# Two weight chunks of a fused attention and MoE kernel converted at earlier places of the first stage

## The chip, the cores and the metric

The kernel runs on one core of one Trainium2 chip. The metric is the device time of one execution in microseconds (us), lower is better. Before the change it is 903.88 us, the median of three runs (903.26 to 904.88).

## The reference

For each of 4 batch entries ("inputs" below) and 8 heads, random-feature attention over 576 positions; then two feed-forward layers, each of them two matrix products with a gate between:

```python
# per head: q, k, v are 576 x 64, omega is 128 x 64
def phi(x):
    h = x @ omega.T - (x * x).sum(-1, keepdims=True) / 2
    return np.exp(h - h.max(-1, keepdims=True)) / np.sqrt(128)
q_p, k_p = phi(q * 64**-.25), phi(k * 64**-.25)
attn = (q_p @ (k_p.T @ v)) / (q_p @ k_p.sum(0) + 1e-6)
x = attn, heads side by side             # 2304 x 512
h = x @ moe_w_in                         # 512 x 2048
x = (h * np.clip(h + 3, 0, 6) / 6) @ moe_w_out
h = x @ moe2_w_in
out = (h / (1 + np.exp(-1.702 * h))) @ moe2_w_out
```

All tensors are float32, and the weights of the two layers arrive in a raw form that the kernel converts on the chip: each chunk goes through a short chain of bit operations and arithmetic, and is then split into a high and a low part, so that one product becomes three matmuls.

## The kernel before

**Stages.** Attention makes x, one input after another; each input has 512 main positions and 64 leftover ones, its 8 heads are held in 4 pairs. The first feed-forward layer is walked in units of (input, chunk), with 16 chunks of 128 hidden columns: `emit_h` multiplies x by the chunk of w_in (line 513, 12 matmuls: 4 blocks of x, one for each pair of heads, by 3), gates the result and splits it, and `emit_o` multiplies it by the chunk of w_out two units later (line 555). The attention of the next input is issued in small steps between the units. The second layer runs last (lines 856 to 1008).

**The steps of one input's attention** (`att_steps`). For head h: PJ(h) projects keys and queries on the features (line 289) and calls `features`, which takes the negated maximum on VectorE (line 295, two per head) and the exponentials on ScalarE (line 297, eight per head); QT(h) transposes the query features, with a copy by VectorE for the first input (line 372); KV(h) sums keys by values and copies the sum by ScalarE (line 363); NU(h) makes the numerator (line 386), and `norm` divides on VectorE (lines 413 to 421); XT(i) transposes a finished pair into one block of x (line 433), split by ScalarE and VectorE (lines 279, 280). For the first input there are 41 steps. The order is PJ(h), NU(h-2), QT(h-1), KV(h-1), and XT(i) after each second head. The loads of a later pair are issued with KV of the odd heads.

**Converting a chunk.** `load_w` loads the raw words of a chunk, two transfers of 512 KB, into one of two buffers `wraw`. `convert_1` does two ScalarE passes (lines 213 and 215), three VectorE passes (lines 217, 221, 225) and one GpSimd multiplication (line 228). `convert_2` adds two halves on VectorE (line 236), copies each to its high part on ScalarE (line 239) and subtracts for the low part on VectorE (line 240); what does not stay resident is stored (line 242). `convert_next(stage, upto, act, dve)` does all conversions up to number `upto` that are not done yet, and then `prefetch_w` issues the raw loads of the two chunks after the last one begun. The buffers `wtop`, `wmag` and `wpow` are single in the first layer, `w` is double.

**What sets the order.** The kernel is written with a planner that gives each instruction to its engine's queue ahead of time, by the order of the program text, by data and buffers, and by its own estimate of durations; at run time each engine takes its queue in that order. An instruction can be planned ahead of earlier text when its inputs are there. `behind(ins)` (line 115) adds one rule: what is issued in its block, and stands on the same engine as `ins`, comes after `ins` in that engine's queue. All loads and stores of this stage are in the one queue of SP, in order.

**Around the change** (lines 743 to 750), while the first input's 41 steps are issued: after the first step at which the third pair of heads (0, 2) has been asked for, that is after KV(1), the raw words of chunks 0 and 1 are asked for, behind that pair's v on SP. Ahead of step 29, KV(5), chunk 0 is converted, with its first ScalarE pass behind the last exponential of the fifth head, its second behind that of the sixth, and its VectorE passes behind the maximum of the fifth head. Chunk 1 is converted after `emit_h(0, 0)`, behind the eighth head's exponentials, chunk 2 after `emit_h(0, 1)`, and so on, `min(c + 2, NC)` chunks after unit c of the first input. From step 29 on the attention of this input takes its PSUM banks from the four of `acc`, and the four of `psp` are left to `emit_h`.

Of the kernel before, what the change touches and what calls it, by code (L numbers as in the profile page):

```python
# [22 lines left out]
def performer_moe_kernel(  # L23
# [26 lines left out]
    NC, _, DM = w1_out.shape  # L50
# [3 lines left out]
    LAG = 2  # L54
    TAIL = 12
    WARM = 8
    FIRST = 4
    ASIDE = 2
    PAIRED = 2
    HELD = 8  # L60
# [54 lines left out]
    def behind(*ins):  # L115
        stack = ExitStack()
        for i in ins:
            if i is not None:
                stack.enter_context(tc.issue_after(i.ins))
        return stack  # L120
# [4 lines left out]
    qkv = {}  # L125
# [74 lines left out]
    def convert_1(l, c, act=None, dve=None):  # L200
        t = wraw.pop((l, c)).rearrange("p (w s) -> p w s", s=4)
        n = 2 * DM
        top = t[:, 1:n + 1, 0]
        mid = t.rearrange("p w s -> p (w s)").bitcast(U32).rearrange("p (w s) -> p w s", s=2)[:, 0:n, 1]
        a = wp.tile([P, n], BF16, tag=f"wtop{l and c % 2}", bufs=1, name="wtop")
        m = wp.tile([P, n], BF16, tag="wmag", bufs=1, name="wmag")
        q = wp.tile([P, n], BF16, tag="wpow", bufs=1, name="wpow")
        w = wp.tile([P, n], F32, tag="w", bufs=2, name="w")

        ab, mb, qb = a.bitcast(I32), m.bitcast(I32), q.bitcast(I32)  # L210
        act = act if isinstance(act, tuple) else (act, act)
        with behind(act[0]):
            nc.scalar.activation(out=a, in_=top.bitcast(BF16), func=AF.Copy, scale=2.0 ** -112)  # L213
        with behind(act[1]):
            nc.scalar.activation(out=w, in_=mid, func=AF.Copy, scale=2.0 ** -36)
        with behind(dve):
            nc.vector.tensor_scalar(
                out=mb, in0=ab, scalar1=3, scalar2=0x7FF87FF8,
                op0=ALU.logical_shift_left, op1=ALU.bitwise_and,
            )  # L220
            nc.vector.scalar_tensor_tensor(  # L221
                out=ab, in0=ab, scalar=-0x7FFF8000, in1=mb,
                op0=ALU.bitwise_and, op1=ALU.bitwise_or,
            )
            nc.vector.tensor_scalar(  # L225
                out=qb, in0=ab, scalar1=-0x7F0080, scalar2=None, op0=ALU.bitwise_and
            )
        nc.gpsimd.tensor_tensor(out=w, in0=w, in1=q, op=ALU.mult)  # L228
        half[l, c] = a, w

    def convert_2(l, c, dve=None):
        a, w = half.pop((l, c))
        for j, kind in enumerate("io"):
            wj = w[:, j * DM:(j + 1) * DM]
            with behind(dve if l == 1 else None):
                nc.vector.tensor_tensor(out=wj, in0=wj, in1=a[:, j * DM:(j + 1) * DM], op=ALU.add)  # L236
            if l == 0:
                s = ws[l, kind, c] = ws_tile(kind, c)
                nc.scalar.copy(s[:, 0], wj)  # L239
                nc.vector.tensor_tensor(out=s[:, 1], in0=wj, in1=s[:, 0].bitcast(F32), op=ALU.subtract)  # L240
                if (l, kind, c) in ws_dram:
                    nc.sync.dma_start(out=ws_dram[l, kind, c], in_=s.bitcast(F32))
        if l == 1:
            whole[c] = w.rearrange("p (k o s) -> p k o s", k=2, o=2)
# [451 lines left out]
    n_load = [0]  # L696
    n_conv = [0, 0]

    def convert_next(stage, upto, act=None, dve=None):

        while n_conv[stage - 1] < min(upto, len(conv)):
            if stage == 1:
                prefetch_w()
                convert_1(*conv[n_conv[0]], act, dve)
            else:
                convert_next(1, n_conv[1] + 1, act, dve)
                convert_2(*conv[n_conv[1]], dve)
            n_conv[stage - 1] += 1
        prefetch_w()

    def prefetch_w():
        while n_load[0] < min(len(conv), n_conv[0] + 2):
            load_w(*conv[n_load[0]])
            n_load[0] += 1
# [25 lines left out]
    att = Att(0, xblk[0], xl)  # L740
    steps = att_steps(att)
    for i, st in enumerate(steps):
        if i == len(steps) - TAIL:
            banks[0] = "acc"
            (a0, d0), (a1, _) = att.feat[FIRST], att.feat[FIRST + 1]
            convert_next(2, 1, (a0, a1), d0)
        st()
        if n_load[0] == 0 and (0, 2) in qkv:
            with behind(last_load[0]):
                prefetch_w()  # L750
    banks[0] = "ps"
# [55 lines left out]
    for u in range(len(units) + LAG):  # L807
        while fetches and fetches[0][0] <= u + AHEAD:
            fetch_w(0, *fetches.pop(0)[1:])
        if u < len(units):  # L810
# [21 lines left out]
            if (n, c) == (B - 1, PREP):  # L832
                assert n_late[0] == len(late)
                prep, _ = x_ops(0, wp, "w")
# [410 lines left out]
```

## Time and profile before

| | us |
|---|---|
| device time, median of three runs | 903.88 |
| device time of the profiled execution | 906.58 |
| its span, first to last instruction | 904.8 |
| TensorE busy (share of the span) | 886.0 (98%) |
| VectorE busy | 554.3 (61%) |
| ScalarE busy | 478.0 (53%) |
| GpSimd busy | 322.6 (36%) |

In the rows PE is TensorE's matmuls, PEld its weight loads, DVE VectorE, ACT ScalarE, POOL GpSimd, SP the queue that issues the loads and stores. L213 is line 213 of the kernel before. A bracket behind a row of the timeline is the idle time of that engine just before the row, and what ended it. An engine that was idle cost nothing unless TensorE, which is busy 98% of the span, had to wait for it.

### The profile page before, as it was taken

The numbers are of one execution on the slowest core, as the hardware profiler recorded it, in microseconds if no ns is written. First come the engines' busy times: TensorE is split into PE (matmuls) and PEld (weight loads), VectorE is DVE, ScalarE is ACT, GpSimd is POOL, SyncE is SP. The second block draws the span as 40 slices with busy tenths as digits, with TensorE's granted clock in tenths as the row PEclk, the third lists the DMA queues.
The fourth block names the chain that finished last, engine by engine and source line by source line (L and its number), as shares of the span: only waits on it lengthen the run. The fifth ranks groups of instructions, "written<-read, shape, count | busy, mean of one in ns | idle before, by whom it ended". The sixth has DMA issues, their size and how long they took to land.

```text
span 904.8 us, 16525 instructions
## 1 busy us (share of the span) xinstructions
PE 886.0 (98%) x6344; PEld 757.1 (84%) x6344; DVE 554.3 (61%) x952; ACT 478.0 (53%) x973; POOL 322.6 (36%) x257
## 2 busy tenths in 40 slices
PE   8899999999999999999999999999999999999998
PEld 6667777788788778878888888878999888899998
DVE  5887688473754736475573343666887343368785
ACT  5887677376664666656553343444545232245452
POOL 0122222044636565475673121877000243440000
PEclk9999999999999999999999999999999999999999
DMA  6677669698888987778857325999889644565562
GB/s 209 226 248 270 234 239 316 245 329 282 286 275 288 342 304 290 233 276 288 314 204 256 128 98 206 349 400 356 277 288 354 233 170 162 180 174 153 158 204 82
DMA packets 74416, 224.57 MB, mean 248 GB/s; under 512 B 7521, under 2 KB 13793, under 8 KB 74337
## 3 DMA queue, kind: packets, MB, share of 16 engines
q1 hardware_dynamic: 73872, 223.12, 71.1%
q8 instruction: 50, 0.82, 0.4%
q10 hardware_dynamic: 464, 0.39, 0.2%
q14 instruction: 30, 0.24, 0.1%
HBM read 160.57 MB, written 62.91 MB: 247 GB/s over the span
## 4 chain that ended last, share of the span: by engine, by line
PE 82%; DVE 8%; ACT 6%; issue 1%; POOL 1%; DMA 1%; DVEq 0%; SPq 0%; ACTq 0%; POOLq 0%
PE o L1008 19%; PE o L555 18%; PE ps L513 18%; PE h L856 16%; PE hl L873 3%; PE ps L289 2%; ACT e L297 2%; DVE w L236 2%; PE ps L386 1%; PE ps L347 1%; ACT wtop L213 1%; DVE mx L295 1%; DVE wtop L221 1%; PE ps L369 1%; DVE gs L530 1%
## 5 line engine op out<-in xcount | busy, mean ns | idle before, releaser
L513 PE MATMUL ps<-x,wss 128*128 128x512 f32 x768 | 195.5, 399 | 2.5 <-ACT el L297 1.1
L1008 PE MATMUL o<-wss,gs 128*128 128x256 f32 x1512 | 173.9, 277 | 0.2 <-DVE gs L977 0.2
L1008 PEld LDWEIGHTS o<-wss,gs 128*128 128x128 f32 x1512 | 173.4, 188 | 0.9 <-DVE gs L977 0.6
L513 PEld LDWEIGHTS ps<-x,wss 128*128 128x128 f32 x768 | 140.9, 189 | 35.0 <-ACT wss L239 3.1
L856 PE MATMUL h<-xo,wss 128*128 128x512 f32 x672 | 158.5, 391 | 0.9 <-DVE t L889 0.9
L856 PEld LDWEIGHTS h<-xo,wss 128*128 128x128 f32 x672 | 123.9, 188 | 27.5 <-DVE t L889 1.8
L228 POOL TENSOR_TENSOR w<-w,wpow 128x1024 f32<-128x1024 f32 x32 | 69.2, 2162 | 204.6 <-DVE wpow L225 166.7
L525 DVE SCALAR_TENSOR_TENSOR ga<-ga,ps 128x512 f32<-128x512 f32 x80 | 50.1, 632 | 121.1 <-ACT ga L524 121.1
L899 POOL TENSOR_TENSOR g<-g,c 128x512 f32<-128x512 f32 x48 | 64.7, 1349 | 164.0 <-ACT g L898 163.8
L976 ACT CAST gs<-g 128x512 fp32r<-128x512 f32 x112 | 69.6, 622 | 80.3 <-PE o L1008 49.3
L555 PE MATMUL o<-gs,wsh 128*128 128x512 f32 (+1 forms) x480 | 110.4, 374 | 1.2 <-ACT gs L529 1.0
L555 PE MATMUL o<-gs,wss 128*128 128x512 f32 (+1 forms) x480 | 109.5, 374 | 0.2 <-ACT gs L529 0.2
L253 POOL TENSOR_TENSOR wsn<-w,wsn 128x512 fp32r<-128x512 f32 x64 | 86.6, 1367 | 63.5 <-ACT wsn L252 63.5
L977 DVE TENSOR_TENSOR gs<-g,gs 128x512 fp32r<-128x512 f32 x112 | 79.9, 716 | 33.6 <-ACT gs L976 32.3
L524 ACT ACTIVATE ga<-ps,three 128x512 f32<-128x512 f32 x80 | 51.4, 650 | 86.5 <-PE ps L513 86.0
L555 PEld LDWEIGHTS o<-gs,wsh 128*128 128x128 f32 x480 | 82.2, 188 | 17.6 <-ACT gs L529 1.4
L555 PEld LDWEIGHTS o<-gs,wss 128*128 128x128 f32 x480 | 82.4, 188 | 15.8 <-ACT gs L529 0.4
L297 ACT ACTIVATE e<-ps,mx 128x128 f32<-128x128 f32 x220 | 61.1, 396 | 23.5 <-DVE mx L295 23.3
L530 DVE TENSOR_TENSOR gs<-ga,gs 128x512 fp32r<-128x512 f32 x80 | 62.5, 791 | 16.5 <-ACT gs L529 14.7
L898 ACT ACTIVATE g<-c 128x512 f32<-128x512 f32 x48 | 30.3, 632 | 60.2 <-DVE c L889 60.2
L529 ACT CAST gs<-ga 128x512 fp32r<-128x512 f32 x80 | 46.0, 580 | 27.8 <-DVE ga L525 27.4
L252 ACT CAST wsn<-w 128x512 fp32r<-128x512 f32 x64 | 38.3, 620 | 39.5 <-DVE w L236 13.2
(132 smaller groups left out, 1102.7 us busy)
## 6 DMA issues: line engine op xcount, KB each, us to landing
wss<-left SPq DMA_DIRECT2D x56, 512.0 KB, 3.9
wss<-ws0i SPq DMA_DIRECT2D x48, 512.0 KB, 4.9
wraw<-in_w_in_dram SPq DMA_DIRECT2D x32, 512.0 KB, 5.4
wraw<-in_w_out_dram SPq DMA_DIRECT2D x32, 512.0 KB, 6.3
left<-wsn SPq DMA_DIRECT2D x32, 512.0 KB, 3.7
wss<-ws0o SPq DMA_DIRECT2D x24, 512.0 KB, 4.6
ws0i<-wss SPq DMA_DIRECT2D x16, 512.0 KB, 3.3
wss<-sumsa SPq DMA_DIRECT2D x16, 512.0 KB, 3.5
```

The source lines that it names most:

```text
L228: nc.gpsimd.tensor_tensor(out=w, in0=w, in1=q, op=ALU.mult)
L253: nc.gpsimd.tensor_tensor(out=s[:, :, 1], in0=t, in1=s[:, :, 0].bitcast(F32), op=ALU.subtract)
L297: act = nc.scalar.activation(out=e[:, r, :], in_=ps[:, r, :], func=AF.Exp, bias=mx[:, r:r + 1])
L513: nc.tensor.matmul(out=ps, lhsT=w[:, wi, kk, :], rhs=x[:, xi, kk, :], start=(m == 0), stop=(m == 3 * NK - 1),)
L524: nc.scalar.activation(out=g, in_=ps, func=AF.Relu, bias=three)
L530: gate[1] = nc.vector.tensor_tensor(out=s[:, 1, :], in0=g, in1=s[:, 0, :].bitcast(F32), op=ALU.subtract)
L555: nc.tensor.matmul(out=ps[:, e, :], lhsT=w[:, wi, cols], rhs=s[:, gi, :], start=(c == 0 and m == 0 and e == 0), stop=(c == NC - 1 and m == ...
L856: nc.tensor.matmul(out=ps, lhsT=s[:, wi, q, :], rhs=xop[q, op][:, xi], start=(first and m == 0), stop=(m == 5), skip_group_check=not first,)
L899: mul = eng.tensor_tensor(out=g, in0=g, in1=src, op=ALU.mult)
L976: split_ins[0] = nc.scalar.copy(hi, g)
L977: split_ins[1] = nc.vector.tensor_tensor(out=lo, in0=g, in1=hi.bitcast(F32), op=ALU.subtract)
L1008: last_row[0] = nc.tensor.matmul(out=out, lhsT=s[:, gi, d * P:(d + 1) * P], rhs=w[:, wi, :], start=(start and m == 0), stop=(stop and m == 2),
```

## The change

The raw words of chunks 0 and 1 are asked for after the first step, behind the v of the second pair of heads (0, 1), since that pair is already asked for then. Chunk 0 is converted as soon as the heads numbered 2 and 3 have their exponentials issued, that is ahead of step 13, NU(1): the first ScalarE pass stands behind the third head's last exponential, the second behind the fourth's, the VectorE passes behind the third head's maximum. The place ahead of step 29 is kept, with the fifth and sixth heads as before, but what is converted there is now chunk 1. After `emit_h(0, 0)` nothing is left to convert; chunk 2 stays after `emit_h(0, 1)`. No instruction is added or taken away.

```diff
-    FIRST = 4
+    SECOND = 4
+    FIRST = 2
...
     for i, st in enumerate(steps):
         if i == len(steps) - TAIL:
             banks[0] = "acc"
+            (a0, d0), (a1, _) = att.feat[SECOND], att.feat[SECOND + 1]
+            convert_next(2, 2, (a0, a1), d0)
+        if n_conv[1] == 0 and FIRST + 1 in att.feat:
             (a0, d0), (a1, _) = att.feat[FIRST], att.feat[FIRST + 1]
             convert_next(2, 1, (a0, a1), d0)
         st()
-        if n_load[0] == 0 and (0, 2) in qkv:
+        if n_load[0] == 0 and (0, 1) in qkv:
             with behind(last_load[0]):
                 prefetch_w()
```

## Rows read from the trace of the kernel before

**Rows 1.** The page, busy time, share and instructions of each engine

```profile
PE 886.0 (98%) x6344; PEld 757.1 (84%) x6344; DVE 554.3 (61%) x952; ACT 478.0 (53%) x973; POOL 322.6 (36%) x257
```

**Rows 2.** Windows: stretch, length, then busy us of each engine

```profile
0.00:60.00 60.00, 50.50 (x591) 39.13 (x592) 44.23 (x102) 42.74 (x118) 9.31 (x13) 1.00 0.71 235
60.00:160.00 100.00, 98.14 (x721) 76.24 (x720) 77.28 (x155) 75.80 (x151) 26.73 (x13) 1.00 0.75 260
```

**Rows 3.** Windows in the first stage: PE, PEld, DVE, ACT, POOL, clock, DMA

```profile
17.00:25.00 8.00, 7.22 (x132) 6.17 (x128) 6.12 (x16) 5.01 (x20) 0.00 (x0) 1.00 0.97 342
25.00:36.00 11.00, 8.60 (x128) 6.64 (x124) 9.19 (x22) 8.66 (x26) 2.14 (x1) 1.00 0.58 199
36.00:52.00 16.00, 13.06 (x149) 9.42 (x148) 13.44 (x37) 12.21 (x28) 4.26 (x2) 1.00 0.76 240
```

**Rows 4.** Waits of PE from 17 to 54 us: total, times, longest

```profile
PE acc L386 <- ACT kv L363: 2.2, 2, 1.5
PE acc L433 <- DVE den L413: 1.5, 2, 0.8
```

**Rows 5.** Groups on DVE from 17.7 to 52 us: busy, mean ns

```profile
L236 DVE TENSOR_TENSOR w<-w,wtop 128x512 f32<-128x512 f32 x5 | 3.3, 688 | 1.2 <-POOL w L228 1.2
L221 DVE SCALAR_TENSOR_TENSOR wtop<-wtop,wmag 128x512 int32<-128x512 int32 x3 | 2.1, 690 | 0.0
L240 DVE TENSOR_TENSOR wss<-w,wss 128x512 fp32r<-128x512 f32 x3 | 2.0, 677 | 0.0
L225 DVE TENSOR_SCALAR wpow<-wtop 128x512 int32<-128x512 int32 x3 | 1.3, 426 | 0.0
L217 DVE TENSOR_SCALAR wmag<-wtop 128x512 int32<-128x512 int32 x3 | 1.3, 423 | 1.0 <-ACT wtop L213 1.0
```

**Rows 6.** Groups on ACT from 17.7 to 52 us, one pass of a conversion

```profile
L215 ACT ACTIVATE w<-wraw 128x1024 f32<-128x1024 uint32 x4 | 4.6, 1188 | 0.5 <-DVE wss L240 0.5
```

**Rows 7.** Timeline of DVE: start, us, then the idle time before

```profile
25.22 0.69 DVE L295 TENSOR_REDUCE mx<-acc 128x4 f32<-128x512 f32 x1 [0.41 <-PE acc L289]
...
31.72 1.29 DVE L236 TENSOR_TENSOR w<-w,wtop 128x512 f32<-128x512 f32 x2 [0.72 <-POOL w L228]
...
40.58 0.43 DVE L217 TENSOR_SCALAR wmag<-wtop 128x512 int32<-128x512 int32 x1 [0.97 <-ACT wtop L213]
...
44.50 1.29 DVE L236 TENSOR_TENSOR w<-w,wtop 128x512 f32<-128x512 f32 x2 [0.45 <-POOL w L228]
```

**Rows 8.** Timeline of POOL, chunk 1's multiplication

```profile
42.34 2.13 POOL L228 TENSOR_TENSOR w<-w,wpow 128x1024 f32<-128x1024 f32 x1 [10.65 <-DVE wpow L225]
```

**Rows 9.** Timeline of PE, one chunk's twelve matmuls

```profile
65.11 3.00 PE L513 MATMUL ps<-x,wss 128*128 128x512 f32 x12
```

**Rows 10.** Timeline of ACT, chunk 2's first high part

```profile
52.60 0.62 ACT L239 CAST wss<-w 128x512 fp32r<-128x512 f32 x1 [1.08 <-DVE w L236]
```

**Rows 11.** Timeline of DVE and POOL, two instructions that lie over each other

```profile
308.70 2.13 POOL L228 TENSOR_TENSOR w<-w,wpow 128x1024 f32<-128x1024 f32 x1 [1.63 <-DVE wpow L225]
...
308.91 2.47 DVE L530 TENSOR_TENSOR gs<-ga,gs 128x512 fp32r<-128x512 f32 x1 [0.35 <-ACT gs L529]
```

**Rows 12.** Timeline of SP, loads of the third pair and of chunk 0

```profile
9.29 0.33 SPq L138 DMA_DIRECT2D qk<-in_qk_dram  x1
...
16.81 0.42 SPq L193 DMA_DIRECT2D wraw<-in_w_in_dram  x1
```

**Rows 13.** DMA issues from 9.2 to 9.4 us: KB, us to landing

```profile
qk<-in_qk_dram SPq DMA_DIRECT2D x1, 512.0 KB, 4.5
```

**Rows 14.** Timeline of PE, the third pair's first projection

```profile
20.98 0.37 PE L289 MATMUL acc<-omt,qk 64*128 64x128 f32 x1
```

**Rows 15.** Windows, the last number is GB/s

```profile
0.00:10.00 10.00, 7.94 (x57) 6.44 (x57) 3.47 (x8) 3.14 (x9) 1.74 (x9) 1.00 0.75 221
20.00:24.00 4.00, 3.60 (x60) 3.02 (x60) 3.13 (x9) 2.28 (x9) 0.00 (x0) 1.00 1.02 399
```

**Rows 16.** Timeline of PE, the transpose of the last pair into x

```profile
50.00 0.63 PE L433 MATMUL acc<-ident,xt 128*128 128x128 f32 x4 [0.67 <-DVE den L413]
```

## The prediction, made before the changed kernel was run

> **What bounds the kernel now.** I read the page first: TensorE is busy for 886.0 us of a span of 904.8 [rows 1]. No view shows work that the change adds to or takes from it, so the time can move only through TensorE's idle time, 18.8 us in all. The windows say where that is: 9.5 us in the first 60 us, 1.9 in the next 100, the remaining 7.4 later [rows 2]. I let the changed stretch begin at 17 us, about where the third head's exponentials end. From 17 to 52 us TensorE is idle for 0.78 + 2.40 + 2.94 = 6.12 us [rows 3]. So 6.1 us is the most that the change can win at its own place.
>
> What makes TensorE wait there is read from its waits: the numerator waits for a copy by ScalarE, the transposes into x wait for VectorE's division [rows 4]. Both engines stand between attention and conversion. VectorE is busy for 28.75 of these 35 us and ScalarE for 25.88, summed from the same windows [rows 3]; VectorE is the nearer bound. I therefore count in VectorE time how early the last block of x (the fourth pair of heads) is finished; its transpose stands at 50.00, after a wait for VectorE [rows 16], and soon after it TensorE is nearly full [rows 2].
>
> **The change part by part.** One chunk costs VectorE 0.423 + 0.690 + 0.426 us in its first half and 2 x 0.688 + 2 x 0.677 us in its second, 1.54 + 2.73 = 4.27 us [rows 5]; ScalarE two passes, the one 1.19 and the other taken alike, and two copies of 0.62, 3.6 us [rows 6, 10]; GpSimd 2.13 us [rows 8]. All of it is moved, none added.
>
> (a) Chunk 0 goes up from 25 to 36 us into about 17 to 25. There VectorE has 8.00 - 6.12 = 1.88 us idle [rows 3], so 4.27 - 1.88 = 2.39 us are left over and push the fourth and fifth heads' chain down. Ends: 0, if the rest falls into idle time of VectorE just after (1.81 us from 25 to 36) or behind TensorE's own work; 4.27, if none of the idle time can be used, since it is there for want of inputs. I take 2.39. ScalarE has 2.99 us idle in that stretch and GpSimd all of it; they cost nothing beside.
>
> (b) Chunk 1 takes chunk 0's old place, from 25 to 36 us: the same instructions, the same neighbours, 0.
>
> (c) From 36 to 52 us chunk 1 is gone: 4.27 us of VectorE, and the two waits that came with it, 0.97 us for ScalarE's first pass and 0.45 for GpSimd [rows 7]. That is -5.69. Ends: -5.69, and -4.27 if other waits take their place.
>
> (d) Chunk 2 is free to move up into the room. Before, its first half stood ahead of the last block and its second behind it. If the second half comes ahead too, the block is 2.73 us later, but three of chunk 2's four blocks can then be multiplied earlier: nine matmuls at 3.00 / 12 = 0.25 us, 2.25 us of TensorE work brought forward [rows 9]. Net 0.48, and 0.45 more if a wait for GpSimd comes with it [rows 7]. Ends 0 and 0.93; I take 0.5, the middle, as nothing points to either.
>
> (e) Chunk 0's new place makes VectorE wait for GpSimd with other work behind. Before, VectorE stood 0.72 us for chunk 0's product, and 1.42 in both waits for chunk 1 [rows 7]. What stands behind the adding instruction on VectorE would be a head's maxima; the exponentials on ScalarE wait for them, and TensorE's transposes wait for those. Ends 0 and 1.42; I take 0.72, the row of the same chunk.
>
> (f) The raw loads go up on SP from 16.81 us [rows 12] to about 5.5, behind the second pair's v. They are 4 x 524,288 bytes = 2.10 MB, and the third pair's load, issued at 9.29 and landed 4.5 us later at 13.8 [rows 12, 13], now has them in front. It is wanted at 20.98 [rows 14], so 7.2 us are to spare. At 399 GB/s, the rate of 20 to 24 us, when such words were on the way, the load lands 5.3 us later, in time; at 221 GB/s, the mean of the first 10 us, 9.5 us later, 2.3 us late [rows 15]. I take 0, by the row of the same kind of transfer; ends 0 and 2.3. Chunk 0's two transfers are first of the four and land well before 17 us. The raw loads of chunks 2 and 3, which wait for a buffer, go up with the conversions, and the load of the fourth pair no longer stands behind four raw loads; chunk 0's store goes up too. No reader of these is late in the trace: 0.
>
> Sum: 2.39 + 0 - 5.69 + 0.5 + 0.72 + 0 = -2.1 us. On the profile's own time, 906.58 (the span of 904.8 and 1.78 around it), that is 904.5. The profiled execution is 2.70 above the median of the runs shown, 903.88, so the same step from the median gives 901.8 us.
>
> The best ends together are 0 - 5.69 + 0 + 0 = -5.7, just under the ceiling of 6.1. The worst, without the load, are 4.27 - 4.27 + 0.93 + 1.42 = +2.4; the late load would come beside a late VectorE, not on top of it.
>
> A wait of VectorE for GpSimd's ports is seen once per meeting in this trace: at 308.91 a VectorE subtraction that lies over GpSimd's multiplication took 2.47 us and ended after the multiplication did [rows 11], where such a subtraction has 0.68 [rows 5], 1.8 us more. By the Trainium skill, "SBUF — State Buffer", section "Who interferes with whom", a VectorE instruction with two SBUF inputs and a GpSimd instruction that reads SBUF exclude each other for the whole of the one that came first. That rule speaks against packing conversions closer, since adding and subtracting are both of that kind; the trace agrees with it at that row.
>
> **The rivals.** A limit on what may be told from the runs: about 0.2%, 1.8 us, is what separates a change from none here.
>
> *Given back at chunk 2.* The last block comes earlier, but chunk 2's high part came at 52.60, after a wait of ScalarE for VectorE [rows 10], and its matmuls were what filled TensorE while chunks 0 and 1 were gated. If chunk 2 is not earlier too, TensorE waits there for as long as was won: 0, 903.9 us. For it: in the next 100 us VectorE is busy for 77.28 and ScalarE for 75.80, so conversions have little room to be ahead [rows 2]. Against it: TensorE is idle for only 1.9 us there, so it does not wait for each conversion.
>
> *The port.* One subtraction of chunk 1 meets chunk 2's multiplication, since both follow chunk 1's adding closely: +1.8 on the sum, 903.6 us. Against it: what lies beside the first stage's multiplications is mostly work that reads PSUM.
>
> *The third pair's load is late.* The raw words run at the early rate, below 2.10 MB / 7.2 us = 292 GB/s: up to +2.3, 904.1 us.
>
> *Slower: chunk 0 stands at the head of VectorE's queue.* Place: 18 to 26 us, where its five kinds of instruction are ahead of the fourth and fifth heads' maxima and divisions, and TensorE has nothing else to do, because the first block of x comes only in that stretch. VectorE's idle time is not usable there (+4.27), both waits are new (+1.42), what chunk 1 leaves is filled by all of chunk 2 (+0.93), and its waits stay (-4.27): +2.4, 906.2 us. It decides from the point at which the fifth or sixth head's maxima, one at 25.22 [rows 7], come some 5 us later than now, since 5.69 - 0.5 is all that comes back. For it: VectorE is the fullest engine, and its order is fixed ahead. Against it: TensorE is 90% busy from 17 to 25, so that much is not on VectorE.
>
> *All in idle time.* Nothing of chunk 0 pushes the heads, (a) and (e) are 0: -5.2, 898.7 us.
>
> **How the numbers follow.** The sum, 0.45, within about 900.4 to 902.9; given back 0.20; the port 0.07; the late load 0.05; chunk 0 in front, slower, 0.15; all in idle time 0.08. The range takes in the sum and all but the far ends of the last two: 898.6 to 906.2. Of the sum's 0.45 some two thirds lie beyond 1.8 us, 0.30, with the 0.08 of the last and a little from the given-back case faster is 0.40; the given-back case, the port and the rest of the sum make 0.38 for no change; slower is chunk 0 in front and what the port, the load and a new order in later stages can add, 0.22.
>
> **What would show it.** (a) VectorE's share from 17 to 25 us near full, and the head that had its maximum at 25.22 some 2 to 3 us later. (c) The last transpose into x [rows 16] 1 to 3 us earlier, with the copy that the numerator waited for no longer behind ScalarE passes of a chunk. (d) Chunk 2's high part earlier than 52.60 by as much. (f) No wait of the third pair's projection for a load. TensorE's idle time in the first 60 us falls from 9.5 to about 7.4, and is unchanged from 60 on. Wrong: the last transpose no earlier than before; or that it is earlier and TensorE's idle time appears between 50 and 160 us; or a difference that lies past 160 us, which my sum does not hold at all.

## The result and the profile after

The changed kernel takes 910.41 us (median of eight runs, 906.28 to 913.9), the kernel before 904.01 beside it on the same chip: ratio 1.0065, 95% interval 1.0042 to 1.0088. By that it is slower by 3.8 to 8.0 us, 5.9 at the ratio itself. 901.8 had been predicted, and 906.2 as the far end of the range.

The profiled execution of the changed kernel was its fastest, 906.28 us at a span of 904.5. The eight runs differ with the clock that TensorE was granted: 906.3 and 908.4 us at a mean of 0.996 of full speed, 908.2 at 0.994, 910.2 to 911.6 at 0.992 (four runs), 913.9 at 0.989. Where a typical execution of the changed kernel is needed, the first experiment has one, with a span of 908.7.

The page of the changed kernel, busy time of each engine, against [rows 1]:

```profile
PE 882.5 (98%) x6344; PEld 758.8 (84%) x6344; DVE 562.3 (62%) x952; ACT 478.0 (53%) x973; POOL 322.9 (36%) x257
```

Its windows, against [rows 2, 3] (PE, PEld, DVE, ACT, POOL, then the granted clock):

```profile
0.00:60.00 60.00, 46.90 (x556) 37.24 (x557) 43.39 (x101) 41.69 (x113) 11.29 (x14) 0.94 0.74 249
60.00:160.00 100.00, 96.67 (x723) 76.92 (x722) 86.47 (x155) 76.26 (x156) 25.05 (x12) 1.00 0.75 267
...
17.00:25.00 8.00, 5.30 (x92) 4.35 (x92) 5.36 (x14) 4.88 (x13) 1.39 (x1) 1.00 0.53 154
25.00:36.00 11.00, 6.55 (x107) 5.59 (x102) 10.00 (x24) 9.28 (x24) 2.88 (x2) 0.92 0.68 248
36.00:52.00 16.00, 13.49 (x140) 10.55 (x139) 13.46 (x31) 12.67 (x33) 3.17 (x2) 0.84 0.85 301
```

Read the PE column first. From 17 to 36 us TensorE is idle for 2.70 + 4.45 us where it was 0.78 + 2.40, and then part of 25 to 52 us runs at the lower of its two clock levels, 1.2 instead of 2.4 GHz (means of 0.92 and 0.84). VectorE is not fuller from 17 to 25 us but emptier, 5.36 against 6.12.

The four transposes into x on PE's timeline, against [rows 16] (line 434 is line 433 of before; the other lines shown are shifted by one too):

```profile
22.23 0.66 PE L434 MATMUL acc<-ident,xt 128*128 128x128 f32 x4 [2.58 <-DVE den L414]
...
33.57 0.63 PE L434 MATMUL ps<-ident,xt 128*128 128x128 f32 x4 [4.05 <-DVE den L414]
...
51.27 0.63 PE L434 MATMUL acc<-ident,xt 128*128 128x128 f32 x4 [0.94 <-DVE den L414]
...
59.21 0.66 PE L434 MATMUL acc<-ident,xt 128*128 128x128 f32 x4
```

Before, the first two of them:

```profile
20.40 0.66 PE L433 MATMUL acc<-ident,xt 128*128 128x128 f32 x4 [0.78 <-DVE den L413]
...
28.99 0.66 PE L433 MATMUL ps<-ident,xt 128*128 128x128 f32 x4 [1.06 <-DVE den L413]
```

The last one has gone from 50.00 to 59.21. The first two waited 0.78 and 1.06 us before; now they wait 2.58 and 4.05. What VectorE did meanwhile, on its timeline:

```profile
18.03 0.43 DVE L218 TENSOR_SCALAR wmag<-wtop 128x512 int32<-128x512 int32 x1 [1.40 <-ACT wtop L214]
18.49 0.69 DVE L222 SCALAR_TENSOR_TENSOR wtop<-wtop,wmag 128x512 int32<-128x512 int32 x1
19.21 0.43 DVE L226 TENSOR_SCALAR wpow<-wtop 128x512 int32<-128x512 int32 x1
19.56 0.68 DVE L296 TENSOR_REDUCE mx<-ps 128x4 f32<-128x512 f32 x1
...
26.55 1.28 DVE L237 TENSOR_TENSOR w<-w,wtop 128x512 f32<-128x512 f32 x2
...
29.09 0.69 DVE L296 TENSOR_REDUCE mx<-acc 128x4 f32<-128x512 f32 x1
...
36.83 1.30 DVE L241 TENSOR_TENSOR wss<-w,wss 128x512 fp32r<-128x512 f32 x2
...
43.72 1.29 DVE L237 TENSOR_TENSOR w<-w,wtop 128x512 f32<-128x512 f32 x2 [1.99 <-POOL w L229]
45.10 0.69 DVE L241 TENSOR_TENSOR wss<-w,wss 128x512 fp32r<-128x512 f32 x1
...
55.87 1.28 DVE L241 TENSOR_TENSOR wss<-w,wss 128x512 fp32r<-128x512 f32 x2
```

And before:

```profile
17.71 0.69 DVE L295 TENSOR_REDUCE mx<-ps 128x4 f32<-128x512 f32 x1 [0.94 <-PE ps L289]
...
47.31 0.68 DVE L240 TENSOR_TENSOR wss<-w,wss 128x512 fp32r<-128x512 f32 x1
...
49.09 0.43 DVE L225 TENSOR_SCALAR wpow<-wtop 128x512 int32<-128x512 int32 x1
```

Chunk 0's first VectorE pass stands at the head of VectorE's queue for 1.40 us, because ScalarE's first pass began only at 16.59, behind the third head's exponentials. The fourth head's maximum, whose inputs were there, comes at 19.56 instead of 17.71. Chunk 0's second half begins only at 26.55, ahead of the sixth head's maximum and of the second transpose. The sixth head's maximum, at 25.22 before [rows 7], comes at 29.09. The pairs of subtractions (line 241) close chunk 1 at 36.83, chunk 2 at 45.10 and chunk 3 at 55.87: ahead of the last transpose stand four chunks and the first half of a fifth, where it was two (the second closed at 47.31) and the first half of a third (at 49.09). The room that chunk 1 left was not given to attention.

One load comes late as well. On the timelines of ScalarE and of TensorE:

```profile
40.52 1.14 ACT L216 ACTIVATE w<-wraw 128x1024 f32<-128x1024 uint32 x1 [2.05 <-DMA wraw<-in_w_out_dram]
41.56 1.12 ACT L298 ACTIVATE e<-acc,mx 128x128 f32<-128x128 f32 x4
...
42.73 1.16 PE L290 MATMUL acc<-omt,qk 64*128 64x128 f32 x14 [1.56 <-ACT e L298]
```

ScalarE stands 2.05 us for the raw words of chunk 2, ahead of the seventh head's exponentials, and TensorE stops 1.56 us for these. In the second trace of this kernel (e0 below) the two are 1.00 and 0.37 us; in e2 and e8 no load is late there and the loss is about the same, so this is not what makes it.

### The profile page after: what moved, and what is told of

The parts are those of the page before. It is cut to its first block, busy times and chain, and to the rows that moved or that the text cites. A ratio compares the mean times of both kernels' runs of the same rounds, so it can differ in the third digit from the quotient of the medians.

```text
span 904.5 us, 16527 instructions
## 1 busy us (share of the span) xinstructions
PE 882.5 (98%) x6344; PEld 758.8 (84%) x6344; DVE 562.3 (62%) x952; ACT 478.0 (53%) x973; POOL 322.9 (36%) x257
## 4 chain that ended last, share of the span: by engine, by line
PE 73%; DVE 12%; ACT 12%; issue 2%; POOL 1%; DVEq 0%; POOLq 0%; ACTq 0%
PE o L1012 19%; PE h L860 16%; PE ps L514 15%; PE o L556 15%; ACT e L298 3%; PE hl L877 3%; ACT wtop L214 2%; DVE w L237 2%; DVE gs L531 2%; DVE mx L296 2%; PE ps L290 2%; ACT w L216 2%; DVE wtop L222 1%; DVE ga L526 1%; ACT gs L530 1%
## 5 line engine op out<-in xcount | busy, mean ns | idle before, releaser
L514 PE MATMUL ps<-x,wss 128*128 128x512 f32 x768 | 189.4, 395 | 0.7 <-ACT el L298 0.4
L556 PEld LDWEIGHTS o<-gs,wsh 128*128 128x128 f32 x480 | 82.0, 188 | 17.7 <-ACT gs L530 1.5
L531 DVE TENSOR_TENSOR gs<-ga,gs 128x512 fp32r<-128x512 f32 x80 | 69.1, 874 | 18.6 <-ACT gs L530 16.8
```

Source lines behind the costliest of these rows:

```text
L514: nc.tensor.matmul(out=ps, lhsT=w[:, wi, kk, :], rhs=x[:, xi, kk, :], start=(m == 0), stop=(m == 3 * NK - 1),)
L531: gate[1] = nc.vector.tensor_tensor(out=s[:, 1, :], in0=g, in1=s[:, 0, :].bitcast(F32), op=ALU.subtract)
L556: nc.tensor.matmul(out=ps[:, e, :], lhsT=w[:, wi, cols], rhs=s[:, gi, :], start=(c == 0 and m == 0 and e == 0), stop=(c == NC - 1 and m == ...
```

## The experiments

Each ran beside the kernel before on the same chip. A span is TensorE's busy time plus its idle time, so the idle time and the time lost at the lower clock (busy time by one minus the granted clock, added up in steps of 1 us) say where a difference lies:

| TensorE, us | idle 17-25 | 25-36 | 36-52 | 52-60 | 60-160 | lost at low clock | ratio to before |
|---|---|---|---|---|---|---|---|
| e1_raws (as before) | 0.78 | 2.58 | 2.75 | 0.06 | 1.87 | 0 | 0.9996 |
| e0_after (the change) | 2.70 | 4.44 | 3.85 | 0.00 | 3.23 | 5.8 | 1.0067 |
| e2_chunk0 | 2.70 | 3.33 | 2.56 | 1.81 | 3.56 | 0 | 1.0063 |
| e8_hold | 2.68 | 3.17 | 1.67 | 1.07 | 2.49 | 3.4 | 1.0058 |
| e15_cut_chunk0 | 1.76 | 3.22 | 2.32 | 2.02 | 3.56 | 4.8 | 1.0062 |
| e16_cut_scalar | 1.90 | 2.56 | 2.32 | 2.03 | 3.56 | 1.6 | 1.0061 |
| e17_cut_both | 0.97 | 1.80 | 2.19 | 0.86 | 2.08 | 0 | 1.0008 |

For e2 the row gives 13.96 - 8.04 = 5.9 us more than e1; its span is 6.2 longer.

**The change again, and its two parts.** e0_after is the changed kernel. e1_raws has only the earlier loads, e2_chunk0 has chunk 0 earlier and chunk 1 back behind the eighth head.

```diff
e1_raws, on the kernel before:
-        if n_load[0] == 0 and (0, 2) in qkv:
+        if n_load[0] == 0 and (0, 1) in qkv:
e2_chunk0, on the changed kernel:
-            (a0, d0), (a1, _) = att.feat[SECOND], att.feat[SECOND + 1]
-            convert_next(2, 2, (a0, a1), d0)
```

> The changed kernel once more, for a second trace. Its one trace so far was of its fastest run (906.28 us, granted clock 0.996), while the median run took 910.41 at a clock near 0.992. Theory (VectorE's order stops TensorE, and the clock falls after the stops): 908 to 913 us, and a trace with more than the 6 us or so at half clock that the first one has between 33 and 48 us, all of it before 160 us; the same three stops at the transposes into x (2.6, 4.1 and 0.9 us). Rival (the extra time lies in later stages, by another order there): half clock or idle time past 160 us that the first trace does not have.

> Only the raw loads go up, behind the second pair; both conversions stay at their old places. VectorE's and TensorE's order are those of before. Theory: the loads cost nothing, 903 to 905 us, the transposes into x at 20.4, 29.0, 40.2 and 50.0 us within 0.5 us. Rival (the raw loads delay the third pair's load, or others): the third pair's projection after 22 us and 906 us or more.

> Raw loads and chunk 0 as in the changed kernel; chunk 1 back behind the eighth head, after the first unit. Theory (chunk 0's pieces ahead of the fourth head's maxima on VectorE do it): the stop of 2.6 us at the first transpose stays, the one at the second shrinks to 1 to 3 us since chunk 0's second half is still ahead of it, 905 to 908 us. Rival (chunk 1 crowding between 25 and 36 us does it): the stops at the second and third transposes go, no fall of the clock, 902 to 904.5 us.

e0: 910.27 us, ratio 1.0067 (1.0043 to 1.0091). e1: 903.2, 0.9996 (0.9985 to 1.0007): the loads cost nothing, and this trace is the clean one for comparisons. e2: 909.77, 1.0063 (1.0046 to 1.008), above the 905 to 908 expected: chunk 0's move alone makes a loss of the same size. The transposes into x of e1:

```profile
20.00 0.66 PE L433 MATMUL acc<-ident,xt 128*128 128x128 f32 x4 [0.78 <-DVE den L413]
28.59 0.66 PE L433 MATMUL ps<-ident,xt 128*128 128x128 f32 x4 [1.07 <-DVE den L413]
...
39.77 0.66 PE L433 MATMUL acc<-ident,xt 128*128 128x128 f32 x4
...
49.60 0.63 PE L433 MATMUL acc<-ident,xt 128*128 128x128 f32 x4 [0.68 <-DVE den L413]
```

And of e2, with the next long stop behind the last one, at a matmul of a chunk:

```profile
22.18 0.66 PE L434 MATMUL acc<-ident,xt 128*128 128x128 f32 x4 [2.58 <-DVE den L414]
32.41 0.63 PE L434 MATMUL ps<-ident,xt 128*128 128x128 f32 x4 [2.94 <-DVE den L414]
...
41.88 0.66 PE L434 MATMUL acc<-ident,xt 128*128 128x128 f32 x4
...
52.13 0.63 PE L434 MATMUL acc<-ident,xt 128*128 128x128 f32 x4 [0.36 <-DVE den L414]
...
56.75 0.73 PE L514 MATMUL ps<-x,wss 128*128 128x512 f32 x2 [1.40 <-ACT wss L240]
```

The table splits e2's loss: 2.7 us from 17 to 36 us, where the first two stops lie (they grew by 1.8 and 1.9, and another wait there went), and 3.4 from 52 to 160 us, in stops such as the last one shown.

**Other places for chunk 0.** e3_maxima puts its VectorE passes behind the fourth head's second maximum; e4_none (from e1) converts nothing within the 41 steps and chunk 0 behind the eighth head; e5_place3 is e2 one head later.

```diff
e3_maxima, on the changed kernel:
-            (a0, d0), (a1, _) = att.feat[FIRST], att.feat[FIRST + 1]
-            convert_next(2, 1, (a0, a1), d0)
+            (a0, _), (a1, d1) = att.feat[FIRST], att.feat[FIRST + 1]
+            convert_next(2, 1, (a0, a1), d1)
e4_none, on e1:
-            (a0, d0), (a1, _) = att.feat[FIRST], att.feat[FIRST + 1]
-            convert_next(2, 1, (a0, a1), d0)
... and behind the loop over the steps:
+    convert_next(2, 1, *att.feat[H - 1])
e5_place3, on e2:
-    FIRST = 2
+    FIRST = 3
```

> The changed kernel with one difference: chunk 0's VectorE passes stand behind the fourth head's second maximum instead of the third's. Theory (the place on VectorE ahead of the maxima does it): the fourth head's exponentials start near 18.5 us instead of 20.3, the stop at the first transpose falls from 2.6 to about 1.5, and the time to 904 to 907 us. Rival (chunk 1 crowding): the first transpose is earlier, the stop of 4 us at the second stays, 908 to 911 us.

> Raw loads early; no conversion inside the 41 steps: chunks 0 and 1 both behind the eighth head. It shows what attention alone takes up to the last transpose into x (49.6 us with chunk 0 behind the fifth head, in the run with the raw loads alone). Theory A (VectorE's time adds up, as the prediction counted it): the last transpose comes 4 to 6 us earlier than 49.6, since chunk 0's 4.3 us and its wait leave. Theory B (attention goes at the pace of its chain from maximum to exponential to transpose, and chunk 0 lay in VectorE's gaps there): at most 2.5 us earlier. Time: TensorE then has no first-layer work until chunk 0 is ready, 905 to 910 us by both.

> Chunk 0 behind the fourth and fifth heads, between the changed kernel's place (third and fourth) and the old one (fifth and sixth); chunk 1 late as before. Theory A (VectorE's sum; the place does not matter much): 908 to 910 us, like chunk 0 behind the third head with chunk 1 late (909.8). Theory B (a place costs what its gaps do not hold; the third head's has none, since VectorE waits for ScalarE's first pass and the maxima wait behind): 903 to 906 us, stops at the first transpose 1 us or less.

e3: 909.52, ratio 1.006 (1.0041 to 1.0079). Its first two transposes wait 1.65 and 2.58 us, less than in the change, and the time does not follow: between the two, TensorE now stops 1.68 us for VectorE's division at the transposes of the fifth head's features. e4: 911.34, 1.0091 (1.0078 to 1.0105): with chunk 0 gone from 25 to 36 us the third transpose comes at 34.89 instead of 39.77, but the last one stays at 49.40, since chunk 0 and most of chunk 1 are then converted ahead of it:

```profile
34.89 0.63 PE L433 MATMUL acc<-ident,xt 128*128 128x128 f32 x4
...
49.40 0.63 PE L433 MATMUL acc<-ident,xt 128*128 128x128 f32 x4 [1.28 <-DVE den L413]
```

e5: 907.2, 1.0049 (1.0037 to 1.0062), between its two theories: the stops at the first two transposes are no longer than in e1 (0.78 and 0.59 us), but TensorE stops 2.65 us at the seventh head's numerator.

**Transposes issued later.** TensorE takes its queue in order, so a transpose that waits also holds the projection behind it. e6_xt_after issues the first input's transposes behind the next even head's projection; e7_xt_raws does that to e1.

```diff
-            if b >= PAIRED and h >= 4 and h % 2 == 0:
+            if (b >= PAIRED or b == 0) and h >= 4 and h % 2 == 0:
...
-            if 2 <= h and h % 2 and (b < PAIRED or h > H):
+            if 2 <= h and h % 2 and (0 < b < PAIRED or h > H):
```

> The changed kernel, with each of the first two transposes into x of the first input issued behind the projection of the next even head instead of ahead of it. TensorE's queue is in order: in the changed kernel it stands 2.6 and 4.1 us at these transposes. If the loss reaches TensorE by these transposes standing ahead of ready projections, the two stops fall under 1.5 us together and the time to 904 to 907 us. If the projections were not ready to be used either (the maxima are late on VectorE), TensorE stops as long at the next transposes of features: 908 to 911 us.

> The raw loads early, conversions at their old places, and the same later issue of the first two transposes into x. Their stops are 0.78 and 1.07 us there. If TensorE's queue order is what costs: 901.5 to 902.5 us. If the stops only move: 903 to 904 us.

e6: 905.59, ratio 1.0029 (1.0016 to 1.0041), by the ratios 3.3 us below the change; e7: 905.77, 1.0032 (1.002 to 1.0045), 3.3 us above e1. On the change the edit gives back about half of the loss, where the first two transposes wait 0.60 and 1.14 us; on e1, where they never waited long, it costs as much (its time fits neither expectation). So how much of the loss reaches TensorE through the waiting transposes cannot be read from the two.

**Holding chunk 2 back.** e8_hold holds it behind the eighth head, where chunk 1 was held before; e9_hold_xt adds e6's edit; e11_35hold has chunk 0 behind the fourth and fifth heads, chunk 1 behind the sixth and seventh. e10_kv6 is another try to beat the kernel before: from e1, chunk 1's ScalarE passes only behind the seventh head's copy of the sum, for which TensorE stops 1.5 us there.

```diff
e8_hold, on the changed kernel:
-                convert_next(2, min(c + 2, NC), *(att.feat[H - 1] if c == 0 else ()))
+                convert_next(2, min(c + 2, NC), *(att.feat[H - 1] if c < 2 else ()))
e11_35hold, on e8:
-    SECOND = 4
-    FIRST = 2
+    SECOND = 5
+    FIRST = 3
e10_kv6, on e1 (kv6 is the seventh head's copy):
+                convert_next(2, min(c + 2, NC), *((att.kv6, att.feat[H - 1][1]) if c == 0 else ()))
```

> The changed kernel, with chunk 2 held behind the eighth head's exponentials and maxima (in the kernel before, chunk 1 was held there). Theory A: the loss is mainly that VectorE's room between 36 and 52 us was filled with chunks 2 and 3 ahead of the last block of x; held back, the last transpose into x starts at 49 to 53 us instead of 59.2, the two first stops of TensorE (2.6 and about 4 us) stay, and the time falls to 904 to 907 us, ratio 1.000 to 1.004. Theory B: the loss is made by the first two stops and the half clock after them, and the refilling is paid back by matmuls of these chunks: time unchanged, 908 to 911 us, ratio 1.005 or more, although the last transpose is earlier.

> The changed kernel with both: chunk 2 held behind the eighth head, and the transposes into x of the first input issued after the projection of the next even head. Theory A (the two losses are separate and add): about 2.5 to 4 us below the later transposes alone (905.6), 901 to 903.5 us, ratio 0.998 to 1.000, not slower than the kernel before. Theory B: as with the later transposes alone, 905 to 907 us.

> The kernel before, with the early raw loads, and chunk 1's ScalarE passes held only behind the copy of the seventh head's sum of keys by values instead of behind the eighth head's exponentials. In the kernel before TensorE stops for 1.5 us at about 42.3 us for that copy, which stands on ScalarE behind these passes. If that stop is taken away and nothing is put in its place: 1.0 to 1.5 us less than the kernel before, ratio 0.9985, the copy's wait gone. Rival: the passes, now ahead of the eighth head's exponentials, hold these up by as much, no change or up to 2 us more.

> The changed kernel with chunk 0 behind the fourth and fifth heads, chunk 1 behind the sixth and seventh, and chunk 2 held behind the eighth. It asks whether one head later is a place where an earlier chunk costs nothing. Theory A (the third head's place is bad because TensorE has only attention to do there and each wait stops it; refilling prevented): the first two stops fall below 1 us each, the last transpose at 50 to 53 us, 902 to 905 us, ratio 0.998 to 1.002. Theory B (a second chunk ahead of the last blocks costs its VectorE time wherever it is put): 906 to 908 us, ratio above 1.003.

e8: 908.2, ratio 1.0058 (1.0046 to 1.007); e9: 907.38, 1.0049 (1.0036 to 1.0062); e10: 909.5, 1.0077 (1.006 to 1.0095); e11: 907.34, 1.0046 (1.0034 to 1.0058). All four expectations of a gain failed; e8, e9 and e11 came out near their second theories, e10 above both of its own. Holding chunk 2 gave nothing on top of e6's edit either (e9 against e6, 1.0049 to 1.0029). e8's four transposes:

```profile
21.61 0.66 PE L434 MATMUL acc<-ident,xt 128*128 128x128 f32 x4 [2.58 <-DVE den L414]
32.94 1.05 PE L434 MATMUL ps<-ident,xt 128*128 128x128 f32 x4 [3.17 <-DVE den L414]
...
45.99 0.66 PE L434 MATMUL acc<-ident,xt 128*128 128x128 f32 x4
...
55.57 0.60 PE L434 MATMUL acc<-ident,xt 128*128 128x128 f32 x4
```

The last transpose is 3.6 us earlier than in the change, yet the intervals of the two ratios overlap: that chunks 2 and 3 filled the room is true, but that this costs the time is not shown. From the third to the last transpose e8 takes 9.58 us, e1 9.83: chunk 2 took the place that chunk 1 had. e10 lost its 1.5 us stop and got others: a matmul of chunk 1 waits 1.72 us for its high part, whose copy came at 47.45 instead of 44.83.

**What VectorE time is worth at either place.** e12 and e13 keep the order of the first stage and change only VectorE's load. e12_add_head4 adds five idle passes ahead of the fourth head's maxima to e1, e13_add_head7 seven behind the seventh head's maxima. e14_cut_chunk1 cuts chunk 1's five VectorE instructions to 64 of 512 columns and lets GpSimd multiply by another tile, so that chunk 1 is not converted; there the planner changed the order too, on VectorE above all, and of one group of seven matmuls and some copies.

```diff
e12, e13, between two steps (the passes go ahead of the next maxima):
...
+            with behind(att.qcopy):
+                for _ in range(5):  # 7 in e13
+                    extra.append(nc.vector.tensor_scalar(
+                        out=dum, in0=dum, scalar1=-0x7F0080, scalar2=None, op0=ALU.bitwise_and))
e14, chunk 1 alone:
+            ab, mb, qb = ab[:, 0:64], mb[:, 0:64], qb[:, 0:64]
-                nc.vector.tensor_tensor(out=wj, in0=wj, in1=a[:, j * DM:(j + 1) * DM], op=ALU.add)
+                nc.vector.tensor_tensor(out=wj[:, 0:64], in0=wj[:, 0:64], in1=a[:, j * DM:j * DM + 64], op=ALU.add)
```

> The kernel before with the early raw loads, and five extra VectorE passes over a scratch tile (128x512, about 0.43 us each, 2.1 us in all; their result isn't used) ahead of the fourth head's first maximum, at about 16.3 us. The order on TensorE, ScalarE and GpSimd is that of the kernel without them. Theory A (VectorE time at this place goes straight to TensorE, which has only attention to do): the fourth head's maximum 1 to 1.5 us later, the first transpose into x waits 1.8 to 2.3 us instead of 0.78, 1 to 3 us more, ratio 1.001 to 1.003. Theory B (step a of the prediction: VectorE's idle time of 1.9 us there takes it): 0 to 0.4 us more.

> The same, but seven extra VectorE passes (3.0 us in all) at about 37 us, behind the seventh head's maxima, where chunk 1 stands in the kernel before; all other orders kept. Theory A (at this place VectorE is not what the end waits for, since TensorE has chunk 0's matmuls to do): under 1 us more. Theory B (step c of the prediction: VectorE time between 36 and 52 us counts one for one): 3.0 us less the 1 us of idle time there, 2 to 3 us more, ratio 1.002 to 1.003.

> The kernel before with the early raw loads; chunk 1's three VectorE passes and two adds work on 64 of 512 columns, and GpSimd multiplies by another tile, so chunk 1 is not converted rightly. It takes about 2.4 us of VectorE out of 36 to 52 us; TensorE's order is the same but for one group of seven matmuls. Theory A (what chunk 1 leaves there is worth little): 0 to 1 us less. Theory B (step c): 2 to 3 us less, 900 to 901 us, ratio 0.997.

e12: ratio 1.0007 (0.9995 to 1.0019), 0.6 us (-0.5 to 1.7) more. e13: 1.0041 (1.0027 to 1.0056), 3.7 us (2.4 to 5.1) more. e14: 1.0011 (1.0001 to 1.0021), 1.0 us (0.1 to 1.9) more, not less. e12 lies between its two theories, e13 speaks against its Theory A, and e14 against both of its own. VectorE's timeline in e12, the added passes and what follows:

```profile
16.34 2.26 DVE L757 TENSOR_SCALAR dum<-dum 128x512 int32<-128x512 int32 x5
18.52 0.68 DVE L298 TENSOR_REDUCE mx<-ps 128x4 f32<-128x512 f32 x1
```

PE's transposes in e12, the first and the last:

```profile
21.20 0.66 PE L437 MATMUL acc<-ident,xt 128*128 128x128 f32 x4 [1.93 <-DVE den L417]
...
51.09 0.63 PE L437 MATMUL acc<-ident,xt 128*128 128x128 f32 x4
```

The maximum moved from 17.32 to 18.52, VectorE's 0.94 us of idle time there having been used, and the first stop grew by 1.15. All that follows in the trace is about as much later, and the last transpose 1.5 us, behind 1.7 us lost at the lower clock; the median is only 1.0 us above e1's by the ratios. In e13 the last transpose moved from 49.60 to 54.01, behind new stops of 1.56 and 2.07 us and 2.9 us lost at the lower clock. In e14 the time cut from VectorE came back as a wait, on its timeline:

```profile
43.82 0.36 DVE L239 TENSOR_TENSOR w<-w,wtop 128x64 f32<-128x64 f32 x2 [2.54 <-POOL w L230]
44.09 1.28 DVE L298 TENSOR_REDUCE mx<-ps 128x4 f32<-128x512 f32 x2
45.29 0.68 DVE L283 TENSOR_TENSOR x<-acc,x 128x512 fp32r<-128x512 f32 x1
```

With less to do, VectorE's order put chunk 1's additions ahead of the maxima of the next input's first head and of the low part of the third block of x, where they wait 2.54 us for GpSimd; the maxima, at 41.70 in e1, come at 44.09, and the low part, for which TensorE waits, at 45.29 instead of 42.90 (0.4 us of each is an offset that this trace has from 20 us on). So time on VectorE between 36 and 52 us counted when something was added, and was not returned when something was taken away and the order changed with it. The cut in e1's own order was not run.

**Chunk 0's work at its new place.** All three are e2. e15 and e16 keep e2's order in the first stage but for small swaps; e17 does so up to about 38 us, from where VectorE's order is another. e15_cut_chunk0 cuts its five VectorE instructions as in e14. e16_cut_scalar cuts ScalarE's two passes to 64 of 1024 columns and leaves VectorE's. e17_cut_both cuts both. Chunk 0 is not converted in any of them.

```diff
e15, e17, chunk 0 alone: e14's cut
e16, e17, chunk 0 alone:
+            nc.gpsimd.memset(a, 0)
+            nc.gpsimd.memset(w, 0)
-            nc.scalar.activation(out=a, in_=top.bitcast(BF16), func=AF.Copy, scale=2.0 ** -112)
+            nc.scalar.activation(out=a[:, 0:64], in_=top.bitcast(BF16)[:, 0:64], func=AF.Copy, scale=2.0 ** -112)
```

> Chunk 0 alone moved up (909.8 us before), with its three VectorE passes and two adds on 64 of 512 columns, and GpSimd multiplying by another tile, so chunk 0 is not converted rightly. About 2.4 us of VectorE less at the third and fourth heads, the wait of VectorE for ScalarE's first pass stays; the order of the first stage is kept. Theory A (the loss is chunk 0's VectorE time and its wait at that place): the first two transposes into x wait 1.5 to 2 us each instead of 2.6 and 2.9, 2.5 to 5 us less than 909.8, 905 to 907 us. Theory B (the loss is in the order around it): 908.5 us or more.

> Chunk 0 alone moved up, with its two ScalarE passes on 64 of 1024 columns (the rest zeros from GpSimd), so chunk 0 is not converted rightly; VectorE's work as it was. About 2 us of ScalarE and the 1.40 us wait of VectorE for the first pass go. Theory A (what counts is ScalarE's first pass, for which VectorE's queue stands ahead of the fourth head's maxima): the maxima 1.2 to 1.4 us earlier than with chunk 0 moved, the first transpose into x waits 1.0 to 1.5 us instead of 2.58, 905 to 908 us. Theory B (the order, whatever its pieces take): the first stop is shorter too, but the time stays at 908.5 us or more, ratio above 1.005.

> The same with both, ScalarE's two passes and VectorE's five on 64 columns. Theory A (work and waits of chunk 0 at that place make the loss): 902.5 to 905 us, ratio below 1.002; the first two transposes into x wait 0.8 to 1.3 us as before the change. Theory B (the order): 907 us or more, ratio above 1.004.

e15: 909.25, ratio 1.0062 (1.0041 to 1.0083). e16: 909.91, 1.0061 (1.0042 to 1.008). e17: 905.5, 1.0008 (0.9993 to 1.0022). Neither half of the work alone moves the time beyond its interval; without both, in e17's order, the loss is gone. The first two transposes, in e15:

```profile
21.40 0.66 PE L437 MATMUL acc<-ident,xt 128*128 128x128 f32 x4 [1.65 <-DVE den L417]
31.52 1.09 PE L437 MATMUL ps<-ident,xt 128*128 128x128 f32 x4 [2.82 <-DVE den L417]
```

in e16:

```profile
21.77 0.66 PE L439 MATMUL acc<-ident,xt 128*128 128x128 f32 x4 [1.90 <-DVE den L419]
31.27 1.09 PE L439 MATMUL ps<-ident,xt 128*128 128x128 f32 x4 [2.56 <-DVE den L419]
```

and in e17:

```profile
20.57 0.66 PE L442 MATMUL acc<-ident,xt 128*128 128x128 f32 x4 [0.97 <-DVE den L422]
29.61 0.66 PE L442 MATMUL ps<-ident,xt 128*128 128x128 f32 x4 [1.47 <-DVE den L422]
```

In e15 and e16 the first stop shrinks by 0.9 and 0.7 us, the second hardly. In e15 VectorE still waits 1.40 us for ScalarE's first pass and 0.72 for the high part, ahead of maxima; in e16 its passes still stand there. What was saved went in these traces into the lower clock (the table), but that is not the whole of it: four of e15's six executions had a mean clock of 0.997 or more, and they took 907.9 to 909.3 us. The later stops stayed as in e2, to 0.3 us; in e17 those between 100 and 145 us, 0.64, 0.71 and 1.89 us in e2, are gone but for one of 0.60.

## Why the prediction was wrong

**The step that failed: (c), "From 36 to 52 us chunk 1 is gone ... That is -5.69."** Nothing of it reached the end of the stage: the last transpose, forecast 1 to 3 us earlier, came 9.2 us later. The place did not stay empty: chunk 2 took it, and chunk 3's work followed. With one of these held back (e8) the stretch between the last two transposes was hardly shorter than in e1, 9.58 us against 9.83. Where a chunk had left its place, the relief was there at the next transpose and gone at the last one: e4's third is 4.9 us earlier than e1's (six of chunk 0's matmuls had left that stretch as well) and its last 0.2; in e2 the stretch from the second to the third takes 9.47 us instead of 11.18, and that from the third to the last 10.25 instead of 9.83. And a cut of chunk 1's VectorE work alone (e14) turned into a wait for GpSimd and 1.0 us more. The row of VectorE's busy time was read rightly, and in e13 3.0 us added there cost 3.7 us, most of it at the lower clock behind new stops. That the time would also come back when taken out was not in that row: behind VectorE's time stand the chain through GpSimd and ScalarE, and the order of the queue decides who gets the room.

**The measure failed with it.** The prediction counted "how early the last block of x (the fourth pair of heads) is finished". The times do not follow that: the last transpose comes at 48.46 in e7 and at 48.26 in e17, earlier than e1's 49.60, and neither is faster than e1; it comes at 52.13 in e2 and at 59.21 in the change, which take the same time within their intervals.

**(a) and (e), 3.1 us together, were too small**, and they named the wrong wait. (a) let 4.27 us of work fall into 1.88 us of VectorE's idle time; (e) saw the wait for GpSimd. In e2 chunk 0 alone moves and its old place is left empty: the prediction's own prices give 3.11 for the new place and 4.27 + 0.72 back for the old one, -1.9 us, and e2 is about 6 us above e1. The new wait was for ScalarE's first pass, 1.40 us at the head of VectorE's queue. ScalarE, costed at nothing, is on the chain of work: followed back in e2's trace, what leads to the second transpose holds chunk 0's two ScalarE passes, 1.03 + 1.01 us, beside 3.97 us of its VectorE work. How the loss divides between them is not shown: with either cut (e15, e16) the loss stayed, and with both cut (e17) it went, but in another order. The first two stops grew by 1.8 and 3.0 us in the change, 1.8 and 1.9 in e2. The lower clock that followed in the change, and the stops of e2 from 52 us on, were in no term.

**(d), +0.5,** had the direction right and the size not: two more chunks, not half of one, came ahead of the last block, which moved by 9.2 us. Their matmuls came forward too, and it cost little: e8, with one chunk less there, is 0.6 us below the change by the ratios, within their intervals.

**(b), 0,** can be read only in e8, where no third chunk interferes: from the second to the third transpose 13.05 us against 11.18 in e1, with most of the difference at the lower clock.

**(f), 0, was right for the third pair's load** (e1), with 2.4 us to spare there instead of 7.2. In the change that load took 8.8 us instead of 4.5 [rows 13] and landed at 19.98; in e7, where its projection is asked for sooner, TensorE waited 1.45 us for it. It was not right for the raw words of chunk 2, of which it said that no reader is late: in the change ScalarE waited 2.05 us for them.

In sum, as bookkeeping, since no run holds (c) by itself: with 0 in place of -5.69 the forecast is +3.6, and new stops and clock beyond (a), (d) and (e) make the other 2.3 to the measured +5.9. The port did not show: in the first 60 us the conversions' additions and subtractions kept their 0.6 to 0.7 us each. Of the rivals, the slower one, chunk 0 at the head of VectorE's queue, had place and sign. It was priced at 906.2, with the relief of (c) still in it, and its point of decision was too far out: the sixth head's maximum came 3.9 us later, not 5. Of what the prediction named as signs against it, the last transpose no earlier than before came true; idle time from 60 to 160 us grew too, to 3.33 us from 1.86.

**Open.** It is not shown how the loss divides between the order of the instructions and the work itself, since e17's order from about 38 us on is not e2's, and e14's is not e1's; nor why e2 has its stops from 52 to 160 us, more than half of its loss. Whether the relief would come if chunk 2 were held until the last block is divided was not tried. No version beat the kernel before: of the thirteen kernels with a changed order and all or nearly all of the work, e0, e2 to e11, e15 and e16, each is 0.3 to 0.9% slower.

## What to carry to other kernels

Time that a moved piece of work leaves free on an engine is not yet time won: here it came back at the next step and was gone a few steps later. First ask which instruction stands next in that engine's queue, and for whom it will wait. Price a moved chain by its hand-overs: each of its instructions that waits at the head of an in-order queue stops everything behind it, also where the engine's busy share has room. Where the bottleneck is 98% busy and the order fixed, try a move with the vacated place filled as it will be filled, not empty.

## What the hardware showed

TensorE's clock fell to its lower level, 1.2 GHz, in or just behind stops of 1.3 to 4.1 us, most of them in the thinly filled first stage: in e0 it fell at about 31 us, inside the second stop (4.05 us, up to 33.73), and the mean granted clock from 25 to 36 us was 0.80, in the window

```profile
25.00:36.00 11.00, 6.56 (x108) 5.56 (x106) 9.54 (x23) 9.27 (x24) 3.03 (x2) 0.80 0.65 245
```

and it did not always do so: in e2's trace, with stops of 2.58 and 2.94 us, it stayed at full speed, while four of its six executions had a mean of 0.994; and a stop of 1.50 us left e1's trace at full speed, while e12's trace lost 1.7 us behind a like one. So the saving from a shorter stop is uncertain by that much from one execution to the next.

The 768 matmuls of `emit_h` with 512 columns (line 513 of before) took TensorE 189.5 us in e0 and 193.9 in e1, 4.4 less. So e0's span is 7.7 us longer than e1's, although its stops and the time lost at the lower clock are 12.0 more. Why the same matmuls took less is not shown.
